# Opening of a pooled-attention plus expert-mix kernel: another order of the first chunk's steps, one block of expert 1 moved back, one weight load cut in three

## The chip, the core and the metric

The kernel runs on one core of one Trainium2 chip. The metric is the device time of one execution in microseconds, the median of several runs. A core has a matrix engine (TensorE, PE in the profile; its weight loads are PEld), a vector engine (DVE), a scalar engine (ACT), GpSimd (POOL) and a queue engine (SP); each works through its own list of instructions in order, and they wait for each other by semaphores. Transfers are issued by POOL, SP and ACT and carried out by 16 DMA engines.

## The reference

`q`, `k` and `v` have 8 batches, 8 heads, 576 positions and 64 columns. Keys and values are averaged over groups of 8 positions (72 remain), each head's attention is taken with them, and the heads side by side make the rows `x` of a mix of four experts.

```python
k_p = k.reshape(B, H, Sp, pool, D).mean(axis=3)
v_p = v.reshape(B, H, Sp, pool, D).mean(axis=3)
attn = softmax(scale * q @ k_p.T)                 # 576 x 72 for each head
x = (attn @ v_p), heads side by side              # 4608 x 512
p = domain_probs / (domain_probs.sum(-1, keepdims=True) + 1e-09)
for e in range(4):                                # w1: 512 x 1024, w2: 1024 x 512
    h = np.maximum(x @ w1[e], 0.0)
    out += p[:, e:e + 1] * (h @ w2[e])
```

## The kernel before

**Chunks.** The rows are worked off in nine chunks of 512: chunk `b` holds the first 512 positions of batch `b`, the ninth the last 64 positions of all batches. For every chunk the attention comes first, then the four experts. The order of all instructions on every engine is the order of the source (a manual schedule; nothing is reordered by a planner).

**Products.** From expert 2 of chunk 0 on, `x @ w1` and `h @ w2` are mostly made by a seven-product scheme on halves of the matrices. `up_product` (L698 on PE) makes one of seven steps of the first product for one of two units; `down` (L766) makes one of seven steps of the second. Both need sums of weight blocks (`first_weight_sums`, `weight_sums`, all through `combine`, L249 on DVE) and sums of activations (`x_sum`, `hidden_sums`). One of these sums, `sums[e][3]`, is written over a block of `w1` itself. Expert 0 and 1 of chunk 0 use plain products for `x @ w1`: `up` makes one of eight blocks of 128 hidden columns from four products 512 wide (L620 on PE, a ReLU on ACT, L625). `down_plain` makes the plain second product for 128 rows from eight products 512 wide (L792), and `add` (L845 on DVE) adds the result into `acc`.

**The opening, `attention_first`.** It is the attention of chunk 0 and the first half of its first product, written out step by step over eight PSUM banks: B2, A2 and W2 with two banks each (`att`, `att_first`, `work_first` in the profile), C0 and C1 with one (`o_ps`).

- `round_q(pair, copy)` (L189) rounds a pair of heads of `q` to bf16 on DVE or ACT; `queries_first` turns that pair with four PE products (L367) and copies the result into `qT` (L368).
- `sum_keys(g, banks)` (36 small PE products, L321) adds up groups of eight keys for four heads, `g` = 0 the low and 1 the high ones; `copy_keys` (L329) copies the two banks into `kpT`, one copy for each. `sum_values` and `cast_values` (L309, L336) do this for the values.
- `scores_first(group, tok, bank)` makes the scores of four heads for one half of the tokens (L548 on PE) and takes their exponential on ACT (L552, 72x1024).
- `context_quarter(t, g, bank)` multiplies with the values (L443) and divides on DVE (L432, L433, giving `x_tok`); `turn_quarter(t, g, bank, copy)` turns that quarter on PE (L458) and copies it into `xT` (L460) on ACT or DVE.
- `up_quarter(t, g, banks)` (L634, eight products 256 wide) multiplies the quarter of `xT` of token half `t` and head half `g` with `w1` of expert 0; `g` = 1 adds onto the sums of `g` = 0 in the same banks and ends with ReLUs on ACT (L640).
- `idle(n, bank, cols)` makes `n` products of zeros (L341), 512 columns wide or 128; nobody reads them.

**Loads.** POOL issues the transfers of k, v and the weights, in the order k, v, `w1` of expert 0 in four parts (the last two with 256 hidden columns), `w1` of 1 and 2 in halves, `w2` of 0 in halves, `w1` of 3, then k, q, `w2` of 1, v, `w2` of 2. They share eight semaphores, so each waits until the transfer issued eight earlier has landed.

**`first_chunk`** writes out the rest of chunk 0. `up(0, 1, (f,))` is block `f` of expert 1, `both(e, step)` is one `up_product` step for both units (two times four products 256 wide), `each(...)` runs sums on DVE. `keys(1, every)` turns the keys of batch 1 on PE (L300) and copies them on ACT (L301); `queries_of_two(pair, ...)` turns four heads of batch 1 (L378) and copies them on ACT (L381). `scores_of_two` makes scores of batch 1 (L396) and their exponentials (L407, L421), `values_folds` adds up its values on DVE (L271, L345), and `context` (L470) uses them, heads 0 to 3 first.

Of the kernel before, what the change touches and what calls it, by code (L numbers as in the profile page):

```python
# [17 lines left out]
def kernel(  # L18
# [13 lines left out]
    E, DM, F = moe_w1.shape  # L32
# [154 lines left out]
    def round_q(pair, copy):  # L187
        hs = slice(2 * pair, 2 * pair + 2)
        copy(out=raws[("q", 0)][:, hs].rearrange("p h r d -> p (h r d)").rearrange(  # L189
                 "p (r h d) -> p r h d", r=NR, h=2),  # L190
             in_=wide_q[:, hs].rearrange("p h (r d) -> p r h d", r=NR))
# [10 lines left out]
    def load_w1(e):  # L202
        if e == 0:
            low, high = slice(0, HK), slice(HK, KC)
            parts = [(low, 0, 2), (high, 0, 2), (slice(0, KC), 2, 3), (slice(0, KC), 3, 4)]
        else:
            parts = [(slice(0, KC), 0, 4)] if e == E - 1 else [(slice(0, KC), 0, 2), (slice(0, KC), 2, 4)]
        for ks, lo, hi in parts:
            fs = slice(lo * F // 4, hi * F // 4)
            nc.gpsimd.dma_start(  # L210
                out=w1_bf[:, e, ks, fs],
                in_=moe_w1[e][:, fs].rearrange("(kc p) f -> p kc f", p=P)[:, ks],
            )
# [101 lines left out]
    def sum_keys(g, banks):  # L315

        for r in range(ROWS):
            for hh in range(2):
                for half in range(2):
                    ps = slice(half * PR, (half + 1) * PR)  # L320
                    nc.tensor.matmul(  # L321
                        banks[half][hh * D:(hh + 1) * D, 0:SP], lhsT=raws[("kraw", 0)][ps, g, hh, r, :],
                        rhs=takes[ps, r], start=(r == 0), stop=(r == ROWS - 1), skip_group_check=True,
                    )

    def copy_keys(g, banks, copies):
        state[("kpT", 0)] = kpTs[0]
        for half, copy in enumerate(copies):
            copy(out=kpTs[0][:, 2 * g + half, 0:SP], in_=banks[half][:, 0:SP])  # L329

    def sum_values(g, banks):
        state[("vp", g)] = list(sum_pool("vraw", g, banks))
# [5 lines left out]
    def idle(n, w_ps, cols=NT):  # L338

        for _ in range(n):  # L340
            nc.tensor.matmul(w_ps[:, 0:cols], lhsT=zeros[:, 0:P], rhs=zeros[:, 0:cols])  # L341
# [15 lines left out]
    def queries_first(pairs, bank, copy):  # L357

        n = len(pairs)
        if pairs[0] == 0:  # L360
            state[("qT", 0)] = apool.tile([P, H, 2, P], BF16, name="qT")
        q_sb, qT = (tile[:].rearrange("p h a t -> p (h a t)").rearrange("p (i r t) -> p i r t", r=NR, t=P)
                    for tile in (raws[("q", 0)], state[("qT", 0)]))
        qt_ps = bank.bitcast(BF16)[:, 0:n * NR * P].rearrange("p (i r t) -> p i r t", r=NR, t=P)
        for i, pair in enumerate(pairs):
            for r in range(NR):
                nc.tensor.transpose(qt_ps[:, i, r], q_sb[:, pair, r], ident[:])  # L367
        copy(out=qT[:, pairs[0]:pairs[0] + n], in_=qt_ps)  # L368
# [189 lines left out]
    def attention_first():  # L558

        B2, A2, W2, (C0, C1) = att, att_first[1], work_first, (bank[:] for bank in chains)  # L560
        vector, scalar = nc.vector.tensor_copy, nc.scalar.copy
        idle(11, W2[:, 0])
        round_q(0, vector)
        round_q(1, scalar)
        queries_first((0,), C0, vector)
        round_q(2, vector)
        round_q(3, scalar)
        idle(1, W2[:, 0])
        queries_first((1,), C1, scalar)
        idle(3, W2[:, 0], P)  # L570
        queries_first((2,), B2[:, 0], vector)
        queries_first((3,), A2[:, 0], scalar)
        idle(1, W2[:, 0])
        sum_keys(0, (C0, C1))
        copy_keys(0, (C0, C1), (vector, scalar))
        idle(4, W2[:, 0], P)
        scores_first(0, 0, B2)
        scores_first(0, 1, A2)
        sum_keys(1, (C0, C1))
        copy_keys(1, (C0, C1), (vector, vector))  # L580
        idle(6, W2[:, 0], P)
        scores_first(1, 0, W2)
        sum_values(0, (C0, C1))
        cast_values(0, vector)
        scores_first(1, 1, B2)
        context_quarter(0, 0, A2)
        sum_values(1, (C0, C1))
        cast_values(1, scalar)
        context_quarter(1, 0, W2)
        turn_quarter(0, 0, A2[:, 0], scalar)  # L590
        context_quarter(0, 1, B2)
        turn_quarter(1, 0, W2[:, 0], scalar)
        up_quarter(0, 0, (C0, C1))
        context_quarter(1, 1, A2)
        turn_quarter(0, 1, B2[:, 0], scalar)
        up_quarter(1, 0, (W2[:, 0], W2[:, 1]))
        turn_quarter(1, 1, A2[:, 0], vector)
        up_quarter(0, 1, (C0, C1))
        up_quarter(1, 1, (W2[:, 0], W2[:, 1]))
        for fc, bank in enumerate((B2[:, 0], A2[:, 0], C0, C1), HF):  # L600
            up(0, 0, (fc,), bank=bank)
# [123 lines left out]
    def weight_sums(e):  # L725
        w, t = w2_bf[:, e], wt_bf[:, e]
        b11, b12 = w[:, LO, 0:HD], w[:, LO, HD:DM]
        b21, b22 = w[:, HI, 0:HD], w[:, HI, HD:DM]
        return [lambda: combine(t[:, 0], b12, ALU.subtract, b11),
                lambda: combine(t[:, 1], b22, ALU.subtract, t[:, 0]),  # L730
                lambda: combine(t[:, 2], b21, ALU.subtract, t[:, 1]),
                lambda: combine(b12, b22, ALU.subtract, b12)]
# [143 lines left out]
    def first_chunk():  # L876


        def each(*pieces):
            for piece in pieces:  # L880
                piece()

        sums = {e: first_weight_sums(e) for e in range(E)}

        def both(e, step):
            for unit in (1, 0) if e == 3 else (0, 1):
                up_product(0, e, unit, step)

        each(*(lambda n=n: x_sum(0, n) for n in range(4)), *sums[0][0:3])
        norm_probs()  # L890
        up(0, 1, (0, 1))
        hidden_sums(0, 0, 0)
        hidden_sums(0, 0, 1)
        up(0, 1, (2, 3))
        each(*sums[1][0:3])
        up(0, 1, (4,), bank=units[0][1][:])
        each(sums[2][0], sums[2][1], sums[2][3], sums[2][2])
        up(0, 1, (5,), bank=chains[0])
        both(2, 0)
        up(0, 1, (6,), bank=chains[1])  # L900
        both(2, 1)
        up(0, 1, (7,), bank=chains[0])
        last_sum = weight_sums(0)
        each(sums[0][3], sums[1][3], *last_sum[0:2])
        both(2, 2)
        down(0, 0, 0)
        both(2, 3)
        hidden_sums(0, 0, 2)
        down(0, 0, 1)
        both(2, 4)  # L910
        hidden_sums(0, 0, 3)
        down(0, 0, 2)
        both(2, 5)
        each(*last_sum[2:])
        down(0, 0, 3)
        both(2, 6)
        each(*sums[3][0:2])
        both(3, 0)
        down(0, 0, 4)
        both(3, 1)  # L920
        each(sums[3][3], sums[3][2])
        fold_keys(1)
        down(0, 0, 5)
        both(3, 2)
        down(0, 0, 6)
        both(3, 3)
        queries_of_two(0, att[:, 0], nc.scalar.copy)
        both(3, 4)
        both(3, 5)
        keys(1, every)  # L930
        queries_of_two(2, chains[0][:], nc.scalar.copy)
        both(3, 6)
        load_w2(3)
        scores_of_two(1, 0, 0)
        down_plain(0, 1, 0)
        lo, hi = slice(0, H // 2), slice(H // 2, H)
        each(*values_folds(1, lo))
        scores_of_two(1, 2, 0)
        fold_first, *fold_rest = values_folds(1, hi)
        fold_first()  # L940
        down_plain(0, 1, 1)
        each(*fold_rest)
        load_wide(0, 0)
        load_q(2)
        load_wide(0, 1)
        load_q_rem(0)
        load_q_rem(1)
        load_wide(1, 0)
        load_wide(1, 1)
        load_wide(1, 2)  # L950
        down_plain(0, 1, 2)
        context(1, 0)
        down_plain(0, 1, 3)
        context(1, 1)
        turn(1, 0)
        hidden_sums(0, 3, 0)
        down_plain(0, 2, 0)
        context(1, 2)
        turn(1, 1)
        hidden_sums(0, 3, 1)  # L960
        down_plain(0, 2, 1)
        context(1, 3)
        turn(1, 2)
        each(*weight_sums(3)[0:3])
        down_plain(0, 2, 2)
        turn(1, 3)
        each(*(lambda n=n: x_sum(1, n) for n in range(3)))
# [162 lines left out]
```

## Time and profile before

| | |
|---|---|
| median of three runs | 489.92 us (489.67 to 490.15) |
| the profiled execution, its time | 490.12 us |
| its span (first to last instruction) | 488.0 us |
| PE busy | 480.0 us, 98% of the span |
| DVE, ACT, POOL busy | 376.7, 303.6, 119.9 us |
| first block of `up` in chunk 0 starts (first L620) | 19.48 us |
| first `up_product` of expert 3 (L698) starts | 39.98 us |
| first `down_plain` of expert 1 (L792) starts | 50.70 us |
| first product of chunk 1's first step (L698, unit 0) starts | 65.49 us |

A timeline line gives start, duration, engine, line of the source, operation, output and inputs, shape, number of instructions merged, and in brackets the idle time of the engine before it with what ended that. PE products overlap: one that is 512 wide is shown with 0.38 us, but the next starts 0.216 us after it (four blocks' lines stand 0.86 us apart for four products); eight that are 256 wide stand 0.87 us apart, four turning products 0.23 us. The profile's own "idle" leaves out what lies inside such an overlap, so a PE wait is read from the distance of starts.

### The profile page before, as it was taken

The page shows a single profiled execution, that of the slowest core. Times are in us where ns is not written, and L with a number is a line of the kernel's source. Part 1 is how long each engine was busy: PE and PEld are TensorE (multiplying, and loading weights), DVE is VectorE, ACT ScalarE, POOL GpSimd, SP SyncE. Part 2 cuts the span into 40 slices and gives each one's busy share as a digit, 9 for nine tenths or more (in the row PEclk, how much of TensorE's full clock was granted, in tenths as well). Part 3 has the DMA queues.
Part 4 walks back from the last instruction along what each step waited for, and adds up shares of the span by engine and source line. Part 5 has one row for each costly group of instructions (what it writes and reads, how often), then busy time and mean ns, then how long its engine had stood idle before and what let it go on. Part 6 is the DMA issues. An engine that isn't in the chain of part 4 may idle for free.

```text
span 488.0 us, 11534 instructions
## 1 busy us (share of the span) xinstructions
PE 480.0 (98%) x4678; PEld 409.1 (84%) x4678; DVE 376.7 (77%) x758; ACT 303.6 (62%) x576; POOL 119.9 (25%) x122
## 2 busy tenths in 40 slices
PE   7999999999999999999999999999999999999996
PEld 4668578898888888888888888888888888888885
DVE  5769799999768976797679866997678766876674
ACT  5677546855676567656765667556755567556650
POOL 8421504242523154016321452111011101010000
PEclk9999999999999999999999999999999999999999
DMA  9999999994977489545954297312111010004003
GB/s 193 203 209 204 205 163 165 101 93 52 116 100 61 80 86 135 37 86 55 157 48 91 27 165 66 69 23 66 34 23 23 23 64 3 12 23 87 1 1 87
DMA packets 104772, 41.96 MB, mean 86 GB/s; under 512 B 75280, under 2 KB 104208, under 8 KB 104720
## 3 DMA queue, kind: packets, MB, share of 16 engines
q0 software_dynamic: 58272, 22.35, 42.1%
q1 hardware_dynamic: 45328, 17.84, 17.1%
q10 hardware_dynamic: 1120, 1.05, 0.6%
q8 instruction: 36, 0.59, 0.5%
q14 instruction: 16, 0.13, 0.1%
HBM read 45.69 MB, written 9.44 MB: 113 GB/s over the span
## 4 chain that ended last, share of the span: by engine, by line
PE 91%; DMA 5%; POOL 1%; ACT 1%; issue 0%; DVE 0%; POOLq 0%
PE unit L698 42%; PE o_ps L766 41%; DMA w_bf<-in_moe_w_dram 5%; PE o_ps L792 3%; PE att L470 2%; PE unit L825 1%; PE att L396 1%; POOL wt_bf L145 1%; PE unit L396 1%; ACT qT L381 0%; PE att L523 0%; PE att L506 0%; ACT H L719 0%; ACT w_bf L713 0%; PE unit L488 0%
## 5 line engine op out<-in xcount | busy, mean ns | idle before, releaser
L845 DVE SCALAR_TENSOR_TENSOR acc<-o_ps,p_all,acc 128x256 f32<-128x256 f32 (+1 forms) x285 | 127.0, 486 | 52.9 <-PE o_ps L766 36.9
L766 PEld LDWEIGHTS <-H 128*128 128x128 bf16 x1320 | 129.0, 98 | 15.6 <-DMA w_bf<-in_moe_w_dram 0.6
L698 PEld LDWEIGHTS <-w_bf 128*128 128x128 bf16 x1088 | 105.1, 98 | 13.1 <-issue 0.2
L678 DVE CUSTOM_DVE_ANT_0 H<-unit,partial 128x512 bf16<-128x512 f32 x128 | 87.2, 684 | 23.8 <-PE unit L698 11.0
L766 PE MATMUL o_ps<-w_bf,H 128*128 128x256 bf16 x792 | 102.6, 273 | 0.4 <-DMA w_bf<-in_moe_w_dram 0.4
L698 PE MATMUL unit<-xT,w_bf 128*128 128x256 bf16 x704 | 100.5, 273 | 0.0
L780 POOL TENSOR_TENSOR acc<-acc,addend 128x512 f32<-128x512 f32 x24 | 30.4, 1265 | 248.0 <-ACT addend L778 200.2
L713 ACT COPY partial<-unit 128x512 f32<-128x512 f32 x128 | 72.2, 591 | 30.3 <-PE unit L698 30.2
L698 PEld LDWEIGHTS <-wu_bf 128*128 128x128 bf16 x816 | 77.5, 98 | 11.7 <-issue 2.5
L698 PE MATMUL unit<-xs,wu_bf 128*128 128x256 bf16 x512 | 77.0, 273 | 0.0
L766 PE MATMUL o_ps<-wt_bf,H 128*128 128x256 bf16 x528 | 68.5, 273 | 0.0
L715 ACT ACTIVATE H<-unit 128x512 bf16<-128x512 f32 x66 | 39.9, 606 | 30.9 <-PE unit L698 30.9
L766 PEld LDWEIGHTS <-S 128*128 128x128 bf16 x528 | 51.6, 98 | 6.0
L719 ACT ACTIVATE H<-unit 128x512 bf16<-128x512 f32 x66 | 39.6, 601 | 25.7 <-PE unit L698 25.4
L711 ACT COPY unit<-unit 128x512 f32<-128x512 f32 x68 | 39.4, 582 | 23.6 <-PE unit L698 18.0
L698 PE MATMUL unit<-xs,w_bf 128*128 128x256 bf16 x256 | 38.4, 273 | 0.0
L155 POOL DMA_DIRECT2D kraw<-in_k_dram x20 | 26.4, 1319 | 42.9 <-DMA kraw<-in_k_dram 42.9
L843 ACT ACTIVATE acc<-o_ps,p_all 128x256 f32<-128x256 f32 x72 | 30.6, 484 | 9.9 <-PE o_ps L766 7.7
L698 PE MATMUL unit<-xT,wu_bf 128*128 128x256 bf16 x240 | 35.7, 272 | 0.0
L766 PE MATMUL o_ps<-wt_bf,S 128*128 128x256 bf16 x264 | 34.2, 273 | 0.0
L766 PE MATMUL o_ps<-w_bf,S 128*128 128x256 bf16 x264 | 34.2, 273 | 0.0
L155 POOL DMA_DIRECT2D vraw<-in_v_dram x20 | 27.5, 1374 | 19.9 <-DMA vraw<-in_v_dram 19.9
(164 smaller groups left out, 501.2 us busy)
## 6 DMA issues: line engine op xcount, KB each, us to landing
out_dram<-acc SPq DMA_DIRECT2D x32, 256.0 KB, 4.7
w_bf<-in_moe_w_dram POOLq DMA_DIRECT2D x10, 512.0 KB, 15.6
q_sb<-in_q_dram POOLq DMA_DIRECT2D x7, 512.0 KB, 10.8
vraw<-in_v_dram POOLq DMA_DIRECT2D x22, 144.0 KB, 6.6
kraw<-in_k_dram POOLq DMA_DIRECT2D x21, 144.0 KB, 6.5
w_bf<-in_moe_w_dram POOLq DMA_DIRECT2D x2, 1024.0 KB, 16.5
w_bf<-in_moe_w_dram POOLq DMA_DIRECT2D x4, 256.0 KB, 8.3
wt_bf<-in_k_dram POOLq DMA_DIRECT2D x4, 144.0 KB, 5.5
```

The costliest lines, as they stand in the source:

```text
L155: nc.gpsimd.dma_start(out=raw[:], in_=rows_of(src, b, 2 * part, 2 * part + 2), accum_op=ALU.add if part else ALU.bypass)
L678: nc.vector._custom_dve(TENSOR_ADD_SAT, out=dst, in0=ps, in1=part, s0=LARGEST, s1=0.0)
L698: nc.tensor.matmul(ps[:, n * HN:(n + 1) * HN], lhsT=lhs[:, kc, f:f + P], rhs=rhs[:, kc, :], start=(not grows and n == 0 and kc == 0), stop ...
L711: nc.scalar.copy(out=banks[1][:], in_=ps)
L713: nc.scalar.copy(out=part[:, step - 2], in_=ps)
L715: nc.scalar.activation(out=quarter(0, 0), in_=ps, func=ACT.Relu)
L719: nc.scalar.activation(out=quarter(0, 1), in_=ps, func=ACT.Relu)
L766: nc.tensor.matmul(ps[:, j], lhsT=lhs[:, i, j * P:(j + 1) * P], rhs=rhs[:, i, :], start=(not grows and i == 0 and j == 0), stop=(i == HF - 1),
L780: nc.gpsimd.tensor_add(out=dst, in0=dst, in1=addend[:])
L792: nc.tensor.matmul(o_ps, lhsT=lhs, rhs=w2_bf[:, e, fc, :], start=(fc == 0), stop=(fc == FCH - 1), skip_group_check=True,)
L843: nc.scalar.activation(out=dst, in_=o_ps, func=ACT.Copy, scale=prob)
L845: nc.vector.scalar_tensor_tensor(out=dst, in0=o_ps, scalar=prob, in1=dst, op0=ALU.mult, op1=ALU.add,)
```

## The change

It does four things, all in chunk 0 or ahead of it.

1. In `attention_first`, the pairs' roundings and turns stand in another order, some idle products are left out, `sum_keys(0)` stands ahead of the turn of the last pair and goes to the two banks of W2, `scores_first(1, 1)` follows `scores_first(1, 0)` directly, both contexts of the low heads stand ahead of `sum_values(1)`, and the end runs `up_quarter(1, 0)`, `turn_quarter(0, 1)`, `up_quarter(0, 1)`, `turn_quarter(1, 1)`, `up_quarter(1, 1)`.
2. `w1` of expert 1 is loaded in three transfers (a quarter, a quarter, a half) where there were two halves; those of experts 2 and 3 as before.
3. In `first_chunk`, block 7 of expert 1 stands behind step 2 of expert 2, and each step of `down(0, 0, ...)` up to 3 stands one step of `both` later. The turn of batch 1's first queries stands behind `both(3, 4)`, not ahead of it.
4. The first halves of `down_plain(0, 1, 0)` and `down_plain(0, 1, 1)` run first, then the second half of row block 0; the second half of row block 1 follows the second pair of scores.

```diff
-            parts = [(slice(0, KC), 0, 4)] if e == E - 1 else [(slice(0, KC), 0, 2), (slice(0, KC), 2, 4)]
+            at = {1: (0, 1, 2, 4), 2: (0, 2, 4), 3: (0, 4)}[e]
+            parts = [(slice(0, KC), lo, hi) for lo, hi in zip(at, at[1:])]
...
         queries_first((0,), C0, vector)
+        round_q(3, scalar)
+        queries_first((1,), C1, scalar)
         round_q(2, vector)
-        round_q(3, scalar)
-        idle(1, W2[:, 0])
-        queries_first((1,), C1, scalar)
-        idle(3, W2[:, 0], P)
         queries_first((2,), B2[:, 0], vector)
+        idle(2, W2[:, 0], P)
+        sum_keys(0, (W2[:, 0], W2[:, 1]))
         queries_first((3,), A2[:, 0], scalar)
-        idle(1, W2[:, 0])
-        sum_keys(0, (C0, C1))
-        copy_keys(0, (C0, C1), (vector, scalar))
-        idle(4, W2[:, 0], P)
+        copy_keys(0, (W2[:, 0], W2[:, 1]), (vector, scalar))
+        idle(4, C0, P)
         scores_first(0, 0, B2)
         scores_first(0, 1, A2)
         sum_keys(1, (C0, C1))
         copy_keys(1, (C0, C1), (vector, vector))
-        idle(6, W2[:, 0], P)
+        idle(5, W2[:, 0], P)
         scores_first(1, 0, W2)
+        scores_first(1, 1, B2)
         sum_values(0, (C0, C1))
         cast_values(0, vector)
-        scores_first(1, 1, B2)
+        idle(6, A2[:, 0], P)
         context_quarter(0, 0, A2)
+        context_quarter(1, 0, W2)
         sum_values(1, (C0, C1))
         cast_values(1, scalar)
-        context_quarter(1, 0, W2)
         turn_quarter(0, 0, A2[:, 0], scalar)
         context_quarter(0, 1, B2)
         turn_quarter(1, 0, W2[:, 0], scalar)
         up_quarter(0, 0, (C0, C1))
         context_quarter(1, 1, A2)
+        up_quarter(1, 0, (W2[:, 0], W2[:, 1]))
         turn_quarter(0, 1, B2[:, 0], scalar)
-        up_quarter(1, 0, (W2[:, 0], W2[:, 1]))
+        up_quarter(0, 1, (C0, C1))
         turn_quarter(1, 1, A2[:, 0], vector)
-        up_quarter(0, 1, (C0, C1))
         up_quarter(1, 1, (W2[:, 0], W2[:, 1]))
...
+        each(sums[2][0], sums[2][1], sums[2][3], sums[2][2])
         up(0, 1, (4,), bank=units[0][1][:])
-        each(sums[2][0], sums[2][1], sums[2][3], sums[2][2])
-        up(0, 1, (5,), bank=chains[0])
         both(2, 0)
-        up(0, 1, (6,), bank=chains[1])
+        up(0, 1, (5,), bank=chains[1])
         both(2, 1)
-        up(0, 1, (7,), bank=chains[0])
+        up(0, 1, (6,), bank=chains[0])
+        both(2, 2)
         last_sum = weight_sums(0)
+        up(0, 1, (7,), bank=chains[1])
         each(sums[0][3], sums[1][3], *last_sum[0:2])
-        both(2, 2)
+        both(2, 3)
         down(0, 0, 0)
-        both(2, 3)
         hidden_sums(0, 0, 2)
+        both(2, 4)
         down(0, 0, 1)
-        both(2, 4)
         hidden_sums(0, 0, 3)
+        both(2, 5)
         down(0, 0, 2)
-        both(2, 5)
         each(*last_sum[2:])
+        both(2, 6)
         down(0, 0, 3)
-        both(2, 6)
         each(*sums[3][0:2])
...
         both(3, 3)
+        both(3, 4)
         queries_of_two(0, att[:, 0], nc.scalar.copy)
-        both(3, 4)
         both(3, 5)
...
         scores_of_two(1, 0, 0)
-        down_plain(0, 1, 0)
+        first, second = range(HF), range(HF, FCH)
+        down_plain(0, 1, 0, first)
+        down_plain(0, 1, 1, first)
         lo, hi = slice(0, H // 2), slice(H // 2, H)
+        down_plain(0, 1, 0, second)
         each(*values_folds(1, lo))
         scores_of_two(1, 2, 0)
         fold_first, *fold_rest = values_folds(1, hi)
         fold_first()
-        down_plain(0, 1, 1)
+        down_plain(0, 1, 1, second)
         each(*fold_rest)
```

## The prediction

> **What bounds the kernel now.** I read the page first, then the chain in order of time, then the timeline of PE from 0 to 70 us with those of ACT, DVE and POOL beside it, and last the transfers' landings.
>
> ```profile
> PE 480.0 (98%) x4678; PEld 409.1 (84%) x4678; DVE 376.7 (77%) x758; ACT 303.6 (62%) x576; POOL 119.9 (25%) x122
> ```
>
> PE is the bound over the whole. Behind 57 us I find no distance of starts over 0.12 us longer than the products need, so nothing there takes up a delay: the end moves by as much as PE is early or late when chunk 1 begins. The edits all lie ahead of that. The chain there:
>
> ```profile
> 16.86 17.82 DMA w_bf<-in_moe_w_dram
> 34.73 1.05 PE o_ps L766 x8
> ```
>
> Up to 34.73 us the chain is a transfer of `w2` of expert 0, which step 1 of `down` waits for. On PE:
>
> ```profile
> 33.33 1.04 PE L698 MATMUL unit<-x_rem,w_bf 128*128 128x256 bf16 x8
> 34.73 1.05 PE L766 MATMUL o_ps<-w_bf,H 128*128 128x256 bf16 x8 [0.36 <-DMA w_bf<-in_moe_w_dram]
> ```
>
> Eight products of 256 need 0.87, so `down` could have started at 34.20: PE loses 0.52 there, and a delay of the opening up to 0.52 is hidden. That is the only slack I find. In the opening, look at the end:
>
> ```profile
> 16.23 0.39 PE L458 MATMUL att<-ident,x_tok 128*128 128x128 bf16 x4
> 16.46 1.04 PE L634 MATMUL work_first<-xT,w_bf 128*128 128x256 bf16 x8
> 16.66 0.58 ACT L460 COPY xT<-att 128x512 bf16<-128x512 bf16 x1 [0.77 <-PE att L458]
> 17.49 0.40 PE L458 MATMUL att_first<-ident,x_tok 128*128 128x128 bf16 x4
> 17.73 1.04 PE L634 MATMUL o_ps<-xT,w_bf 128*128 128x256 bf16 x8
> 17.93 0.42 DVE L460 COPY xT<-att_first 128x512 bf16<-128x512 bf16 x1 [0.49 <-PE att_first L458]
> ```
>
> Between a turn (L458) and the end of its copy (L460) lie 16.66 + 0.58 - 16.23 = 1.01 us on ACT, 17.93 + 0.42 - 17.49 = 0.86 on DVE. Each time PE makes an `up_quarter` of another quarter meanwhile (0.87): the copy is covered.
>
> **The change part by part.** The working follows the profiled execution (490.12 us; the median shown is 0.20 lower).
>
> *The end of the opening* (edit 1). `up_quarter(0, 1)` now directly follows `turn_quarter(0, 1)` and reads just what that turn's copy writes. PE spends 0.23 on the turn, then waits: 1.01 + 0.06 - 0.23 = 0.84 (0.06 is what lies between a DVE result and the PE product that waits for it, 17.44 to 17.49 at the last turn). `up_quarter(1, 1)` likewise follows `turn_quarter(1, 1)`: 0.86 + 0.06 - 0.23 = 0.69. Nothing else stands behind them on PE that could go ahead. The wait of 0.16 at 17.49 (17.33 would have done) goes, since `x_tok` is long ready. Sum 0.84 + 0.69 - 0.16 = +1.37.
>
> *The start of the opening* (edit 1).
>
> ```profile
> 7.64 0.40 PE L367 MATMUL att<-ident,q_sb 128*128 128x128 bf16 x4 [0.25 <-DVE q_sb L189]
> 8.30 0.59 ACT L368 COPY qT<-att_first 128x512 bf16<-128x512 bf16 x1 [0.45 <-PE att_first L367]
> 8.98 0.22 ACT L329 CAST kpT<-o_ps 128x72 bf16<-128x72 f32 x1
> 9.33 0.40 PE L548 MATMUL att<-qT,kpT 64*128 64x256 bf16 x4
> ```
>
> The turn at 7.64 waits for DVE's rounding (to 7.59) and stays there. Behind it now come two idle products (0.11) and the key sums (0.42), so the last turn stands near 8.43, not 7.88. Its ACT copy starts 0.42 after it (8.30 - 7.88), at 8.85, and ends at 9.44; ACT's key copy queues behind it and ends near 9.57 where it ended at 9.20. The first scores wait for that: 9.62 to 9.70, +0.3. From there the chain of copies and exponentials is as before; having both contexts early saves 0.2 at the second turn (14.87 - 13.81 = 1.06 falls to 0.85, the two divisions then running without a gap on DVE). At the first `up_quarter` (15.10) I take +0.22; bounds 0 and +0.5.
>
> The left-out idle products, 2 x 0.216 + 13 x 0.056 against 17 x 0.056, are 0.2 us less work, all where PE waits anyway: 0. *One rule weighs against leaving them out.* The eleven of the start take 4.0 us, where 11 x 0.216 = 2.4 would do at the later pace: a slow PE costs 1.65 over such a stretch, though the granted clock is shown as 1.00. In this trace PE stays fast through a gap of 0.95 us; the change makes gaps of 0.8, 0.7 and 0.8. I take 0, and +1.65 as the upper end. The Trainium skill, "TensorE: Matmul & The Clock Gate", section "Part 1: The HAM clock gate", has the clock halved after an idle window of about 3.4 us; by that these gaps cost nothing; its section on a second failure mode says that frequent short idling can do it too, which would add the upper end.
>
> *The weight load in three* (edit 2). One more issue on POOL, 0.73 to 0.86 us by the rows of L210, and all later POOL transfers use the next semaphore. POOL is ahead: from 14.29 on it waits for landings (0.35, 1.83, 0.82 us), and issues lie 17 us before their landing. The queue is busy throughout, and small parts are not slower: the two quarters of expert 0 were 8.7 and 9.2 us under way, issued 0.75 apart, so they landed 1.25 apart; halves (11.0 and 12.9, issued 0.73 apart) 2.6. 0; without the lead, up to 0.86.
>
> *Steps moved back in chunk 0* (edit 3). `down` step 1 gets one more step of 0.87 ahead of it and comes 1.59 late from the opening: it starts at 36.66, 2 us after the landing. The 0.52 goes: **-0.52**. On DVE the sum that overwrites `w1` of expert 1 must wait until block 7 has been multiplied (30.72 before; 0.87 later by the order, 1.59 by the opening, 1.03 long: 34.2); behind it are queued two sums for `wt` (0.69 each), one for H, and the first `relu_sum`s. The first that PE needs is the second `wt` sum, done near 36.4, for step 2 at 38.4: covered by 2 us, 0.
>
> The turn of batch 1's queries moves behind `both(3, 4)`:
>
> ```profile
> 46.16 0.61 PE L378 MATMUL att<-ident,q_sb 128*128 128x128 bf16 x8
> 47.15 1.04 ACT L381 COPY qT<-att 128x1024 bf16<-128x1024 bf16 x1
> 48.11 1.09 ACT L719 ACTIVATE H<-unit 128x512 bf16<-128x512 f32 x2
> 49.60 1.05 ACT L381 COPY qT<-o_ps 128x1024 bf16<-128x1024 bf16 x1
> 50.70 1.89 PE L792 MATMUL o_ps<-w_bf,H 128*128 128x512 bf16 x8
> ```
>
> ACT runs unbroken from the first copy (47.15) to the second's end (50.65), and `down_plain` waits for that bank. The turn ended at 46.77, so ACT was 0.34 late for it. Now the turn ends at 46.77 + 0.87 - 0.10 = 47.54 (two ACT waits, 0.10 near 42 us, go with the later `down` step 3) and ACT starts 0.04 later: 47.58 - 47.15 = **+0.43**; bounds -0.1 and +0.6.
>
> *`down_plain` in halves* (edit 4).
>
> ```profile
> 52.68 0.75 DVE L845 SCALAR_TENSOR_TENSOR acc<-o_ps,p_all,acc 128x512 f32<-128x512 f32 x1 [1.70 <-ACT expT L421]
> 56.43 0.29 DVE L345 TENSOR_TENSOR vp<-wt_bf 72x256 bf16<-72x256 bf16 x1
> 56.52 0.54 PE L470 MATMUL att<-vp,expT 72*128 72x65 bf16 x8
> ```
>
> DVE's first `add` waits for the whole of `down_plain(0, 1, 0)`. From it DVE works without a gap to the last value sum (56.72), which the second half of `context` (56.77) waits for. Row block 0 now ends after twelve products, not eight: the `add`, and all value sums queued behind it, come 4 x 0.216 = 0.86 later, while PE reaches `context` after the same amount of work. No slack covers it: **+0.86**; lower bound 0, if DVE caught up.
>
> Sum: 0.22 + 1.37 - 0.52 + 0.43 + 0.86 = **+2.36**: 492.48 for the profiled execution, 492.3 against the median.
>
> **The rivals.** *Part of it hidden.* If the second half of `context` does not wait (term of edit 4 at 0) and ACT's chain is as before (0), +1.1: 491.0; with one of the two, 491.5 to 491.9. For it speaks that DVE is idle for 1.70 just ahead; against, that what it waits for is the very thing that is moved.
>
> *PE falls back to its slow pace* in the opening: +2.36 + 1.65 = 494.0. For it: the first stretch's pace; against: the gap of 0.95 that did nothing.
>
> *Not slower.* The wait for `w2` is the only one that decides, and the copies of the opening are through before their products, as they would be if a copy ended 0.23 after its turn began. Then PE gains the 0.52 and can gain more, but only up to the next transfer:
>
> ```profile
> w_bf<-in_moe_w_dram POOLq DMA_DIRECT2D x1, 1024.0 KB, 21.2
> ```
>
> `w1` of expert 3, issued at 18.42, lands at 39.6, and its first step runs at 39.98: 0.36 is all that can be gained up to there. With the waits around the scores gone as well (0.10 at 50.03, 0.24 at 50.70, 0.12 at 56.77), -0.8: 489.1. Against it stand the copy rows: 1.01 and 0.86.
>
> *The change does not do what it says:* the first block of `up` stands no more than 0.52 later, and edit 4's wait is covered; then 489.9, no change.
>
> **How the numbers follow.** About 0.2% (0.98 us) is what a measurement of this kernel can tell from no change. Forecast 0.67; partly hidden 0.17; slow PE 0.08; not slower 0.04; no change 0.04. The forecast's own bounds: the start of the opening 0 to +0.5, ACT's chain -0.1 to +0.6, the copies 0.1 less each: 491.3 to 492.8. The range reaches down to 491.1, near the lower end of the partly hidden cases, and up to a PE that is slow for two thirds of such a stretch (493.4); left out are that lower end (0.03), most of the slow PE (0.05) and the last two cases (0.08): 0.16. Faster than 0.2%: the not-slower case ends at -0.8, so only a fraction of it, 0.02. Within 0.2%: the rest of it, no change and a tail of the partly hidden, 0.07. Slower 0.91.
>
> **What would show it.** In the profile after: PE waits of some 0.8 and 0.7 for L461 (ACT, then DVE) ahead of L634 near 18 and 20 us; the first L620 near 21.1 where it was at 19.48; no PE wait for `w2`; the first L698 of expert 3 near 41.1; `down_plain` near 52.2; a wait of some 0.9 for the last value sum in the second half of `context`; from there a constant lag. I am wrong if the first L620 stands before 20, if products of 512 columns stand 0.43 apart behind 6 us, or if the lag does not stay.

## The result and the profile after

The changed kernel takes 492.44 us (median of 6 runs, 492.40 to 492.62), the kernel before 490.03 us beside it (6 runs, 489.67 to 490.23): a ratio of 1.0051, 95% interval 1.0038 to 1.0064, slower by 2.4 us. The profiled execution took 492.62 us with a span of 490.8 us; the one of before took 490.12 with 488.0. One profiled execution further down (run c1_steps_folds_first) ran at a granted clock of 0.948 and took 502.68 us, so its trace is not compared. Line numbers of the changed kernel are one higher than before up to about L560 and the same from L600 to L890.

The page, PE's busy time and the share of each engine in the chain that ended last:

```profile
PE 480.7 (98%) x4680; PEld 410.0 (84%) x4680; DVE 376.9 (77%) x758; ACT 303.9 (62%) x576; POOL 120.8 (25%) x123
PE 95%; DVE 2%; ACT 1%; issue 1%; POOL 1%; POOLq 0%
```

PE does the same work, and the transfer of `w2` is gone from the chain (it had 5%). The chain now runs through PE from the opening on, and through DVE's value sums ahead of the first context. In the timeline the end of the opening reads:

```profile
17.63 0.39 PE L459 MATMUL att<-ident,x_tok 128*128 128x128 bf16 x4
18.05 0.59 ACT L461 COPY xT<-att 128x512 bf16<-128x512 bf16 x1 [1.64 <-PE att L459]
18.69 1.03 PE L634 MATMUL o_ps<-xT,w_bf 128*128 128x256 bf16 x8 [0.67 <-ACT xT L461]
19.56 0.39 PE L459 MATMUL att_first<-ident,x_tok 128*128 128x128 bf16 x4
19.98 0.42 DVE L461 COPY xT<-att_first 128x512 bf16<-128x512 bf16 x1 [2.02 <-PE att_first L459]
20.46 1.03 PE L634 MATMUL work_first<-xT,w_bf 128*128 128x256 bf16 x8 [0.51 <-DVE xT L461]
```

No `up_quarter` stands between a turn and the one that needs its copy, so PE waits twice: 18.69 - 17.63 - 0.23 = 0.83 us and 20.46 - 19.56 - 0.23 = 0.67. The start:

```profile
7.86 0.40 PE L368 MATMUL att<-ident,q_sb 128*128 128x128 bf16 x4 [0.45 <-DVE q_sb L189]
9.15 0.59 ACT L369 COPY qT<-att_first 128x512 bf16<-128x512 bf16 x1 [1.12 <-PE att_first L368]
9.63 0.22 ACT L330 CAST kpT<-work_first 128x72 bf16<-128x72 f32 x1
9.91 0.39 PE L549 MATMUL att<-qT,kpT 64*128 64x256 bf16 x4 [0.57 <-ACT kpT L330]
```

The keys had been summed by 8.72, but ACT's key copy is queued behind its copy of the last turn, and the first scores wait for it. Further down, `down` step 1 and the two ACT copies of batch 1's queries:

```profile
36.06 1.04 PE L698 MATMUL unit<-x_rem,wu_bf 128*128 128x256 bf16 x8
36.94 1.03 PE L766 MATMUL o_ps<-w_bf,H 128*128 128x256 bf16 x8
...
48.93 1.01 ACT L382 COPY qT<-att 128x1024 bf16<-128x1024 bf16 x1 [0.39 <-PE att L379]
51.33 1.05 ACT L382 COPY qT<-o_ps 128x1024 bf16<-128x1024 bf16 x1
52.43 2.75 PE L792 MATMUL o_ps<-w_bf,H 128*128 128x512 bf16 x12 [0.30 <-ACT qT L382]
```

At 36.94 PE comes 0.88 after the step before it, without a wait. `down_plain` still waits for the second copy, which ends at 52.38. Last, the first context:

```profile
55.28 0.75 DVE L845 SCALAR_TENSOR_TENSOR acc<-o_ps,p_all,acc 128x512 f32<-128x512 f32 x1 [3.04 <-issue]
59.02 0.29 DVE L346 TENSOR_TENSOR vp<-wt_bf 72x256 bf16<-72x256 bf16 x1
58.26 0.29 PE L471 MATMUL att<-vp,expT 72*128 72x65 bf16 x4
59.37 0.29 PE L471 MATMUL att<-vp,expT 72*128 72x65 bf16 x4 [0.82 <-DVE vp L346]
```

The first `add` comes 2.60 later than before, 0.87 more than the start of `down_plain` (52.43 against 50.70), and PE waits 0.98 between the halves of the context. Behind it every PE product is 2.59 us late, the same amount to the end of the kernel.

### The profile page after: what moved, and what is told of

The parts are those of the page before. It is cut to its first block, busy times and chain, and to the rows that moved or that the text cites. A ratio compares the mean times of both kernels' runs of the same rounds, so it can differ in the third digit from the quotient of the medians.

```text
span 490.8 us, 11536 instructions
## 1 busy us (share of the span) xinstructions
PE 480.7 (98%) x4680; PEld 410.0 (84%) x4680; DVE 376.9 (77%) x758; ACT 303.9 (62%) x576; POOL 120.8 (25%) x123
## 3 DMA queue, kind: packets, MB, share of 16 engines
q10 hardware_dynamic: 1120, 1.05, 0.6%
## 4 chain that ended last, share of the span: by engine, by line
PE 95%; DVE 2%; ACT 1%; issue 1%; POOL 1%; POOLq 0%
PE unit L698 42%; PE o_ps L766 41%; PE o_ps L792 2%; PE att L471 1%; PE unit L825 1%; PE o_ps L620 1%; PE att L397 1%; PE unit L620 1%; PE unit L397 0%; DVE wt_bf L272 0%; POOL wt_bf L145 0%; PE work_first L634 0%; PE o_ps L634 0%; ACT qT L382 0%; PE att L524 0%
## 5 line engine op out<-in xcount | busy, mean ns | idle before, releaser
L698 PEld LDWEIGHTS <-w_bf 128*128 128x128 bf16 x1088 | 105.2, 98 | 13.1 <-issue 0.2
L698 PE MATMUL unit<-xT,w_bf 128*128 128x256 bf16 x704 | 100.4, 273 | 0.0
L698 PEld LDWEIGHTS <-wu_bf 128*128 128x128 bf16 x816 | 77.6, 98 | 11.7 <-issue 2.5
L698 PE MATMUL unit<-xs,wu_bf 128*128 128x256 bf16 x512 | 77.0, 273 | 0.0
L698 PE MATMUL unit<-xs,w_bf 128*128 128x256 bf16 x256 | 38.4, 273 | 0.0
L698 PE MATMUL unit<-xT,wu_bf 128*128 128x256 bf16 x240 | 35.7, 272 | 0.0
```

What stands on the lines that cost most here:

```text
L698: nc.tensor.matmul(ps[:, n * HN:(n + 1) * HN], lhsT=lhs[:, kc, f:f + P], rhs=rhs[:, kc, :], start=(not grows and n == 0 and kc == 0), stop ...
```

## The experiments

All ratios are against the kernel before, on the same chip, with 95% intervals. The table lists landmarks of each profiled execution in us: the first scores, the first L620, the first L698 of expert 3, the first L792, the distance of starts of the two halves of the first context, and the first L698 of chunk 1. In the traces of c2, c3 and d1 the record of the first L620 is missing; the value given is the start of the next block of four less 0.864, the distance of blocks.

| run | ratio | scores | L620 | exp. 3 | L792 | halves | chunk 1 |
|---|---|---|---|---|---|---|---|
| before | 1 | 9.33 | 19.48 | 39.98 | 50.70 | 0.25 | 65.49 |
| after | 1.0051 | 9.91 | 21.33 | 41.30 | 52.43 | 1.11 | 68.08 |
| a1_end_back | 1.0017 | 9.70 | 19.79 | 39.75 | 50.89 | 1.12 | 66.55 |
| a2_plain_back | 1.0027 | 9.70 | 21.12 | 41.09 | 52.22 | 0.25 | 67.01 |
| a5_folds_early | 1.0024 | 9.71 | 21.13 | 41.10 | 52.23 | 0.13 | 66.91 |
| a4_keys_on_vector | 1.0043 | 9.06 | 20.79 | 40.76 | 51.89 | 1.11 | 67.55 |
| a3_queries_back | 1.0035 | 9.91 | 21.33 | 41.30 | 51.95 | 1.11 | 67.61 |
| b1_end_only | 1.0012 | 9.55 | 20.91 | 40.87 | 51.59 | 0.25 | 66.39 |
| b2_steps_only | 1.0001 | 9.32 | 19.36 | 39.32 | 49.98 | 0.87 | 65.60 |
| b3_load_only | 0.9996 | 9.50 | 19.51 | 39.92 | 50.65 | 0.50 | 65.68 |
| c2_folds_first | 0.9999 | 9.34 | 19.45 | 39.41 | 50.14 | 0.14 | 65.08 |
| c3_mended | 1.0000 | 9.06 | 19.48 | 39.45 | 50.10 | 0.45 | 65.62 |
| d1_steps_short_sums | 0.9988 | 9.33 | 19.50 | 39.56 | 50.23 | 0.13 | 64.91 |

### One part of the change undone at a time

**a1_end_back**: each turn is again a step ahead of the `up_quarter` that reads it.

```diff
-        up_quarter(1, 0, (W2[:, 0], W2[:, 1]))
         turn_quarter(0, 1, B2[:, 0], scalar)
-        up_quarter(0, 1, (C0, C1))
+        up_quarter(1, 0, (W2[:, 0], W2[:, 1]))
         turn_quarter(1, 1, A2[:, 0], vector)
+        up_quarter(0, 1, (C0, C1))
```

> The changed kernel with the old order at the end of the opening alone (the two turns and two up_quarters as before). Theory, that PE waited there for the copies of xT: the two waits of 0.84 and 0.68 go, the one of about 0.16 for x_tok comes back or not; the first block of up stands 1.2 to 1.4 us earlier (near 20.0), nothing behind it takes that back, since step 1 of down (36.94) and the first step of expert 3 (41.30) then still stand later than their weights land (34.6 and 39.5): 1.2 to 1.4 us faster than the changed kernel, 1.0 to 1.2 slower than the kernel before. Rival, that the weight transfers set the time of chunk 0: at most half of it arrives at the end, and a wait for a transfer shows on PE.

Measured: 491.10 us, 1.0017 [1.0006, 1.0029]. From the first `up_quarter` (15.41) to the first L620 (19.79) it takes 4.38 us, as before (19.48 - 15.10); in the changed kernel 5.71 (21.33 - 15.62). The order at the end costs 1.33 us.

**a2_plain_back**: `down_plain(0, 1, 0)` and `(0, 1, 1)` whole and in the old order.

> The changed kernel with down_plain(0, 1, 0) and (0, 1, 1) whole again, as before. Theory, that the value sums queue on DVE behind an add that waits for twelve products: the wait of 0.98 in the second half of context falls to about 0.1, 0.85 to 0.9 us faster than the changed kernel (+1.5 to +1.6 against before). Rival, that DVE is late for another reason (the values' landing at 53.1 to 53.5, or the exponentials on ACT): the wait stays above 0.5.

Measured: 491.58 us, 1.0027 [1.0016, 1.0038]. The halves of the context stand 0.25 apart as before, and from L792 to chunk 1 it takes 14.79 us (15.65 in the changed kernel): 0.86 us.

**a5_folds_early**: the halves stay, but the value sums are queued on DVE ahead of the `add` that waits for row block 0.

```diff
-        down_plain(0, 1, 0, second)
         each(*values_folds(1, lo))
+        down_plain(0, 1, 0, second)
```

> The changed kernel with the sums of the first half of the values ahead of the add of down_plain(0, 1, 0) in DVE's queue; PE's order is that of the change. Theory, that only the place in DVE's queue makes the wait: DVE does them in the 3 us in which it was idle, the wait of 0.98 in context falls under 0.15, 0.85 to 0.95 us faster than the changed kernel, as much as when the halves are undone. Rival, that the halves of the products themselves cost it (more changes of bank, the order on PE): no more than 0.3 faster.

Measured: 491.44 us, 1.0024 [1.0014, 1.0035]; 14.68 us from L792 to chunk 1. The halves cost nothing in themselves: what costs is DVE's queue, in which the value sums stand behind the later `add`.

**a4_keys_on_vector**: the second copy of the low keys on DVE, `(vector, vector)` for `(vector, scalar)`.

> The changed kernel with both key copies of the low heads on DVE, so that none queues on ACT behind the copy of the last turn. Theory: DVE has both done near 9.25, the first scores stand near 9.4 where they stood at 9.91, and 0.3 to 0.5 us of it reach the first block of up and the end: 0.3 to 0.5 faster than the changed kernel. Rival, that the scores wait for the turns and copies of the queries or that later steps of the opening wait for the values' transfers: first scores as late as before, or under 0.15 us at the first block of up.

Measured: 492.24 us, 1.0043 [1.0031, 1.0056]. In its timeline the key copies and the first scores no longer stand behind ACT:

```profile
8.63 0.37 DVE L330 CAST kpT<-work_first 128x72 bf16<-128x72 f32 x2
8.94 0.59 ACT L369 COPY qT<-att_first 128x512 bf16<-128x512 bf16 x1 [1.30 <-PE att_first L368]
9.06 0.39 PE L549 MATMUL att<-qT,kpT 64*128 64x256 bf16 x4
```

The first scores come 0.27 ahead of the kernel before; the second ones still wait for ACT's copy of the last turn (to 9.53) and stand at 9.57, where they stood at 9.54. The first `up_quarter` (15.08) is 0.33 earlier than in a1, a2 and a5 (15.41), which differ from it in nothing up to there but the key copy, and 0.02 ahead of the kernel before: the ACT queue is the whole cost of the new order of the start. (The changed kernel itself had it at 15.62, for a reason given in the last section.) This rests on the traces: the ratios of this run and of the changed kernel differ by 0.0008, some 0.4 us, which is less than their intervals.

**a3_queries_back**: `queries_of_two(0, ...)` ahead of `both(3, 4)` again.

> The changed kernel with the turn of batch 1's first queries ahead of both(3, 4) again. Theory, that the chain of four copies on ACT starts when this turn ends: the way from the first step of expert 3 to down_plain falls by 0.4 (11.13 to about 10.7), and 0.4 us faster than the changed kernel. Rival, that the gain turns into a longer wait for the value sums behind it: none at the end.

Measured: 492.15 us, 1.0035 [1.0022, 1.0048]. From expert 3 to L792 it takes 10.65 us, 11.13 in the changed kernel, 10.72 before: 0.48 us comes from ACT's chain.

### One part of the change alone

**b1_end_only**: the kernel before with only the new order at the end of the opening.

> The kernel before with the new order at the end of the opening alone. Theory: 1.34 us later at the first block of up, of which the wait of 0.52 for the second half of w2 takes up all it has: 0.8 to 0.85 slower than the kernel before, and no PE wait for w2. Rival, that the opening is hidden behind the weight transfers: no slower than 0.2; rival, that the wait does not give way: 1.3.

Measured: 490.95 us, 1.0012 [1.0003, 1.0021]. The first L620 is 1.43 late (0.10 of it ahead of the first `up_quarter`), expert 3 0.89, chunk 1 0.90. The difference of 0.54 is the wait for `w2`: the delay uses up the only slack that the prediction found.

**b2_steps_only**: the kernel before with only the steps moved back in chunk 0 (block 7 of expert 1 after step 2 of `both(2, ...)`, `down` one step later), the queries' turn left in place.

> The kernel before with the moved steps of chunk 0 alone (block 7 behind step 2 of expert 2, down up to step 3 one step later; the queries' turn stays). Theory: the 0.52 for w2 goes, but the weights of expert 3 land at 39.6 and hold its first step (39.98 before) to a gain of 0.33; two ACT waits of 0.10 near 42 go as well: 0.3 to 0.45 faster than the kernel before, with a PE wait of about 0.2 for w1. Rival, that no transfer holds it: 0.6 faster. Rival, that DVE's sum over w1, now later, is what PE waits for: no gain.

Measured: 490.14 us, 1.0001 [0.9989, 1.0014]. No gain can be told; the interval by itself would still allow the 0.3 to 0.45 us that were expected, but the trace shows where they went. The wait for `w2` is gone and expert 3 starts 0.66 earlier, yet chunk 1 starts 0.11 later than in the kernel before. The transfers landed up to 1.06 us earlier in this execution than in the one of before (`w1` of expert 3 at 38.55, not 39.61), so PE did not wait for `w1` either. What holds it is in the timeline of DVE and PE:

```profile
53.45 1.14 DVE L271 TENSOR_TENSOR wt_bf<-wt_bf 72x1024 bf16<-72x1024 bf16 x2 [0.53 <-DMA wt_bf<-in_v_dram]
56.54 0.29 DVE L345 TENSOR_TENSOR vp<-wt_bf 72x256 bf16<-72x256 bf16 x1
56.88 0.29 PE L470 MATMUL att<-vp,expT 72*128 72x65 bf16 x4 [0.58 <-DVE vp L345]
```

DVE waits for the last 64 KB of batch 1's values, which landed at 53.35 us, and PE for the value sums made from them. In the kernel before they landed at 53.16, just ahead of DVE, which came from an `add` and did not wait:

```profile
53.35 1.13 DVE L271 TENSOR_TENSOR wt_bf<-wt_bf 72x1024 bf16<-72x1024 bf16 x2
```

**b3_load_only**: the kernel before with only `w1` of expert 1 loaded in three parts.

> The kernel before with the load of expert 1's w1 in three parts alone. Theory: the landings of w2 and of expert 3's weights move by no more than 0.1, within 0.1 us of the kernel before. Rival, that the added issue and the next semaphore push later transfers back: landings 0.3 to 0.8 later, and as much slower, since the wait for w2 stands on the path.

Measured: 490.24 us, 0.9996 [0.9987, 1.0004]. `w1` of expert 3 lands at 39.55 (before 39.61); the load in three costs and gains nothing that can be told.

### Is there a floor under the kernel before?

**c1_steps_folds_first** and **c2_folds_first**: b2 and the kernel before, each with the last value sums ahead of the `add` of row block 1.

```diff
         fold_first()
-        down_plain(0, 1, 1)
         each(*fold_rest)
+        down_plain(0, 1, 1)
```

> The steps moved in chunk 0 alone, and beside them the last two value sums of batch 1 ahead of the add of row block 1 on VectorE (PE's order is the one of the run with the steps alone). In that run PE was 0.66 us ahead at the first step of expert 3 and lost it to a wait of 0.77 us in the first context. There the value sums began at 53.45 us, when the last part of the values had landed, and needed 1.14 + 0.33 + 0.60 + 0.45 + 0.29 us and an add of 0.66 between them. Theory, the add in the queue makes the wait: without it the last sum ends near 56.2 us where it ended at 56.83, the wait falls to about 0.15 us, the first product of chunk 1 stands near 65.0 us (65.5 in the kernel before), and the time is 0.4 to 0.6 us below the kernel before. Rival, the landing alone makes it: it moves with PE and the wait stays at 0.6 or more; no difference from the kernel before. A second rival: w1 of expert 3 lands near 39.6 us again, not at 38.55, so that PE waits for it and only 0.0 to 0.2 us is gained.

> The kernel before, with only the two value sums ahead of the add. Theory: the second half of its first context waits 0.12 to 0.15 us for the last sum, which now ends near 56.1 us where it ended at 56.72; 0.1 us faster, within what can be told from no change. Rival, the add that now comes later holds up the bank that PE uses next: a new wait behind the context and up to 0.5 us slower.

Measured: c1 490.19 us, 0.9998 [0.9989, 1.0007] (not in the table); c2 490.27 us, 0.9999 [0.9991, 1.0008]. No gain from taking the `add` out of the way of the sums can be told; the intervals reach 0.5 and 0.4 us below the kernel before, where c1 was expected. The trace of c2 is of an execution in which the transfers landed early (`w2` at 33.76, the values at 52.87): chunk 1 starts at 65.08, 0.41 ahead of the kernel before, and its 489.70 us is the lowest of eleven.

**c3_mended**: the changed kernel with the four costly parts undone (a1, a2, a3, a4) and the same edit.

> The changed kernel with each part undone that a run showed to cost something (the old order at the end of the opening, the second copy of the low keys on VectorE, the queries' turn ahead of step 4 of expert 3, whole row blocks in the plain down products) and with the two value sums ahead of the add; what stays of the change is the opening's order up to there, the load in three and the steps moved. From the measured differences: 2.4 less 1.34, 0.33, 0.43, 0.86 and 0.1 to 0.6 leaves 0.1 to 1.2 us below the kernel before; with the transfers' landings as bounds (w1 of expert 3 at 38.5 to 39.6, values at 53.2 to 53.5) I expect 0.4 to 0.6 us below it, equal to the run of the steps with the sums ahead. Rival: the parts do not add up, since slow first products and landings set the pace; no difference from the kernel before.

Measured: 490.24 us, 1.0000 [0.9991, 1.0009]. All of the 2.4 us is back; the 0.4 to 0.6 us below the kernel before did not come. Its timeline shows why:

```profile
53.48 1.14 DVE L272 TENSOR_TENSOR wt_bf<-wt_bf 72x1024 bf16<-72x1024 bf16 x2 [0.65 <-DMA wt_bf<-in_v_dram]
56.24 1.40 DVE L845 SCALAR_TENSOR_TENSOR acc<-o_ps,p_all,acc 128x512 f32<-128x512 f32 x2
56.38 0.29 PE L471 MATMUL att<-vp,expT 72*128 72x65 bf16 x4 [0.16 <-DVE vp L346]
57.03 1.89 PE L792 MATMUL o_ps<-w_bf,H 128*128 128x512 bf16 x8 [0.37 <-DVE acc L845]
```

The wait for the sums is shorter, but now the next `down_plain` waits for the `add` that empties its bank. From the landing at about 53.4, DVE owes the value sums and one `add`, some 3.4 us; in either order PE goes on at about 57.0 (57.01 in b2, 57.03 here). From DVE's start on these values to that block of PE it takes 3.55 or 3.56 us in the kernel before, b2, b3, c2 and c3 alike. What moves is the start, with the landing: 52.94 in c2, where PE went on at 56.50, 53.53 in b3, where it did at 57.09.

**d1_steps_short_sums**: b2 with 1.05 us less for DVE in that stretch.

```diff
-        fold_first, *fold_rest = values_folds(1, hi)
-        fold_first()
+        fold_rest = values_folds(1, hi)[2:]
```

> The steps moved in chunk 0 alone, with two of VectorE's value sums left out: for the upper four heads of batch 1 the sums over rows 2 to 7 of each pool are not made, so those pooled values hold 2 rows of 8. This takes 0.60 + 0.45 us out of VectorE's queue between the landing of the values and the first context and changes nothing on PE or in the transfers. Theory, a floor: from the landing of the last values (53.2 to 53.5 us) VectorE needs about 3.4 us for the value sums and one add, whichever is first, and PE cannot be past the first context before 56.9; the gain of the moved steps (0.66 us) ends there. With 1.05 us less in that queue the wait of 0.77 falls to below 0.15, the first product of chunk 1 stands 0.5 to 0.7 us before the one of the kernel before, and the time is 0.4 to 0.7 us lower. Rival: the gain of the steps is only a matter of when w2 of expert 0 lands (33.7 to 34.7 us by run), the kernel before has it too in most of its runs; then the wait is short, but the time is within 0.2 us of the kernel before.

Measured: 489.52 us, 0.9988 [0.9977, 0.9998], with 490.25 for the kernel before beside it:

```profile
53.66 1.14 DVE L271 TENSOR_TENSOR wt_bf<-wt_bf 72x1024 bf16<-72x1024 bf16 x2 [0.70 <-DMA wt_bf<-in_v_dram]
56.06 0.42 PE L470 MATMUL att<-vp,expT 72*128 72x65 bf16 x8
56.32 1.89 PE L792 MATMUL o_ps<-w_bf,H 128*128 128x512 bf16 x8
```

The values landed no earlier than in b2, yet the context runs through, PE goes on 0.69 earlier than in b2 and chunk 1 starts at 64.91. With less work for DVE behind the landing the gain of the moved steps arrives, 0.1 to 1.1 us by the interval. So the floor is the landing of batch 1's values plus DVE's work on them; it lies as early or as late as the values land. The gain here is bought with sums that are left out; of the kernels that make them all, none can be told from the kernel before by its median.

## Why the prediction was right

The forecast was 492.3 us within 491.1 to 493.4, and slower with a chance of 0.91; 492.44 was measured. Its terms:

| step | predicted | by the two traces | by a run |
|---|---|---|---|
| start of the opening (first `up_quarter`) | +0.22 | 15.62 - 15.10 = +0.52 | a4, a1 |
| end of the opening | +1.37 | 5.71 - 4.38 = +1.33 | a1: 1.33 |
| load in three | 0 | none seen | b3: 0 |
| wait for `w2` | -0.52 | (41.30 - 21.33) - (39.98 - 19.48) = -0.53 | b1, b2 |
| ACT's chain for the queries | +0.43 | 11.13 - 10.72 = +0.41 | a3: 0.48 |
| DVE's queue ahead of the context | +0.86 | 15.65 - 14.79 = +0.86 | a2: 0.86, a5: 0.97 |
| sum | +2.36 | +2.59 | c3: all back |

**The mis-sized term** is the start of the opening. Two things were missed. First, 0.21 of it is PE's pace, not the order: in the profiled execution of the changed kernel the turn at 7.64 stood at 7.86, and in a1, a2 and a5, where it stood at 7.64 again, the first `up_quarter` came at 15.41, +0.31. Secondly, the step "from there the chain of copies and exponentials is as before" is wrong by 0.2: the scores came at 9.70 in a1, the upper end of what was worked out (9.62 to 9.70), but the value sums now stand behind the fourth scores and not the third (third scores 11.21, 10.89 before; sums 11.65, 11.12 before), and the first turn came 14.34 - 13.81 = 0.53 late, of which the second turn got 0.22 back, as forecast. +0.31 remains. The +0.22 does not follow from the two numbers beside it in the prediction: +0.3 at the scores less 0.2 at the second turn is some +0.1. With the pace the term is +0.52, just beyond its upper bound of +0.5.

**Landmarks.** The first L620 was put near 21.1 (21.33), expert 3 near 41.1 (41.30), L792 near 52.2 (52.43): all late by some 0.2, the pace. The wait in the context was put at some 0.9 (0.98), and the lag behind it is constant. That the median came within 0.1 of the forecast is in part luck: the terms of the two traces add up to +2.59, the medians differ by 2.41, and the profiled execution, 492.62, is the slowest of the six.

**The rivals.** Nothing was hidden: a2 and a5 gave back 0.86 and 0.97, a3 the ACT term. PE did not fall back to its slow pace: eight products of 256 columns took 0.87 as before behind the waits of 0.83 and 0.67 us, and those of 512 stood 0.216 apart behind the one of 0.98. For such waits the Trainium skill, "TensorE: Matmul & The Clock Gate", section "Part 1: The HAM clock gate", has no cost, since it names an idle window of about 3.4 us; these three waits agree with it. They show nothing of the falling back that its section "A second HAM failure mode: psum-queue depth-cycling" tells of for frequent short idling; three waits in 41 us do not settle how frequent it would have to be.

**The "not slower" rival was priced by the wrong step.** It let PE gain until `w1` of expert 3 lands and put the best case at 489.1. In b2 and c3 PE started expert 3 at 39.3 to 39.5 without waiting for `w1`, and no gain could be told in the time: in their traces it ended at the values of batch 1 and DVE's sums. The step failed in taking for a limit the next transfer on the chain of before, when that chain ran through DVE 15 us later with DVE only 0.2 us behind a landing. The forecast is not touched by this, because the changed kernel is behind that floor by more than 2 us and its -0.53 counts in full.

## What to carry to other kernels

Putting a consumer right behind the step that makes its input costs the whole round trip through the copying engine (here 0.83 us on ACT, 0.67 on DVE), unless other work of the same engine stands between them. When a product is cut and interleaved, look at what is queued on the vector engine behind its first result: work that has nothing to do with it comes late by the same amount, and moving that work ahead in the queue gives it back. Before a wait is taken away, find the next landing that any engine near the chain waits for, and add that engine's work after it; here the gain ended there.

## What the runs showed of the hardware that was not expected

**PE's first pace ends at different times.** The first products 512 wide follow each other in 0.427 us. In seven of the thirteen traces compared this changed to 0.216 at 4.6 to 5.2 us (before, a2, a4, b2, c2, c3, d1). In a1 and a5 all eleven idle products were slow, and the turns at 6.40 were fast. In the other four (after, a3, b1, b3) these turns were still slow, 0.107 apart for 128 columns and not 0.056, until 6.8 to 7.2 us. Up to 6.4 us before, b1, b2, b3, c2 and d1 run the same instructions. The granted clock is shown as 1.00 in the stretches either way. In the changed kernel the eleven idle products at the start take 4.88 us, in the kernel before 4.19. The price at the first `up_quarter` was 0.21 in the new order (15.62 in after and a3, 15.41 in a1, a2 and a5). In the old order it was 0.2 at most: 15.13 and 15.20 with a late change (b3, b1), 14.99 to 15.12 with an early one (b2, c2, before, d1). The Trainium skill, "TensorE: Matmul & The Clock Gate", section "Part 1: The HAM clock gate", describes a free-running window of about 3.4 us, gives half a microsecond either way for the change of pace, and also tells of one kernel with 6, 11 or 14 slow products by run; the executions here, from 4.6 to about 7.2 us, go with the second and not with the half microsecond. In the changed kernel PE had been at work without a gap from 1.26 to 6.1 us and was still slow, so 4 us of products, the least that the page's section "Why this matters for your kernels" advises for warming up, would not have done there.

**The same transfer lands up to 1 us earlier or later.** The second half of `w2` of expert 0 landed at 33.65 (b2) to 34.68 (before), `w1` of expert 3 at 38.55 to 39.61, in kernels with the same loads. The `w2` transfer took 17.8 us from issue to landing in both; it was issued at 15.85 in the one and 16.86 in the other, each time when POOL had waited for an earlier landing (1.17 and 1.83 us). So a wait of half a microsecond for a landing, read from one profile, need not be there in the next: c2, which changes nothing ahead of 53 us, had no wait for `w2` (33.76). No difference between medians was seen to come from this, but single executions may show it: c2's profiled one, with early landings, was the lowest of its eleven.
